# q and k of the attention stage turned by VectorE in 32x32 blocks instead of by TensorE

## The chip, the cores and the metric

The kernel runs on one core of a Trainium2 chip. The metric is the device time of one execution in microseconds; of several runs the median is given. A core has TensorE (PE; its weight loads are listed apart as PEld), VectorE (DVE), ScalarE (ACT), GpSimd (POOL) and SyncE (SP), which issues nearly all DMAs here. The DMAs run on 16 DMA engines of the core.

## The reference

```python
# q, k, v: (4, 12, 448, 64) fp32
scores = q @ k.T / sqrt(64) - log(448)
attn   = sigmoid(scores)
x      = (attn @ v)  -> (4 * 448, 768)          # tokens by features

# first mixture of experts: 8 experts, 768 -> 1024 -> 768
compute = x @ w_skip > 0
e       = argmax(x @ w_gate); g = softmax gate of e
out     = x;  out[compute] = x + g * relu(x @ w1[e]) @ w2[e]

# second mixture: experts by cosine with expert_emb / tau, every token computed
out = g2 * relu(x @ v1[e2]) @ v2[e2]
```

## The kernel before

It has two parts. The attention stage takes the first 178 us; the two mixtures of experts take the rest. The change is in the first part, and at the stores of the second.

**Attention.** The work is cut into 12 units (`duos`), each of one batch and four heads. A unit holds two pairs of heads, i = 0 and 1; j = 0 and 1 is the head in a pair. Head pairs lie in the two halves of the 128 partitions, so that q and k of a pair, once turned, are tiles `qT` and `kT` of 128 rows (two heads of 64 features) by 448 tokens. The keys of a head are cut into `NH` = 7 pieces of `KT` = 64. So a unit has 7 steps, and there are 84 steps in all, numbered g. In a step,

- `score(w, h)` runs four matmuls (both pairs, both heads) into one tile `psS`, and ScalarE takes the sigmoid of all of it into a tile `A`;
- `av(w, h)` runs four matmuls of the values with the tile `A` of two steps earlier (`LAG` = 2), summed in two PSUM tiles `psO` over the 7 steps. After the last step of a unit `take_x` moves them to `xT`, one by VectorE and one by ScalarE.

Each engine runs its instructions in the order in which the code issues them. SP has one queue. A DMA also waits for the DMA eight places ahead of it in this queue, since eight semaphores are used in turn.

**Loads.** `load_qk(w)` loads q and k of a unit by eight DMAs of 112 partitions x 4 pieces of 64 floats, `load_v(w)` the values by four DMAs of 64 partitions x 7 pieces of 64 floats. Tokens of q stand in the order (p c): partition p holds the four tokens 4p to 4p + 3. So the rows of the result stand in that order too, and the kernel's later index tables (`rid`) and stores follow it. The tiles `k`, `q` and `v` have two buffers each. In unit w, step 0 issues `load_qk(w + 1)` and step 2 issues `load_v(w + 1)`, whose buffer was that of unit w - 1.

**Transposes.** `prep(w, nm)` turns q or k of one unit: eight transposes of 112x128 by TensorE into two PSUM banks `ps_t`, which VectorE (i = 0) and ScalarE (i = 1) copy to `qT` or `kT`. For unit 0 this stands ahead of the first step; for unit w + 1 it stands in step 3 (k) and step 4 (q) of unit w, between `score` and `av`.

**Routing.** After the last unit of a batch the steps of the next unit also hold the first mixture's router for that batch (`route_stages`): matmuls, two groups of transposes and chains of small VectorE operations.

**Experts.** `dense` runs one expert over a whole batch; its weights come by SP in units of 256 columns (`load1`, `load2`, tile `r`). `finish` turns the result back to rows (tile `row`) and stores it: three batches by one DMA each of 112 rows of 12 KB, the last by two DMAs.

Of the kernel before, what the change touches and what calls it, by code (L numbers as in the profile page):

```python
# [10 lines left out]
F32 = mybir.dt.float32  # L11
F32R = mybir.dt.float32r
I32 = mybir.dt.int32
AF = mybir.ActivationFunctionType
# [7 lines left out]
def sigmoid_attention_moe_moe_kernel(  # L22
# [15 lines left out]
    nc = tc.nc  # L38
# [3 lines left out]
    P = 112  # L42
# [48 lines left out]
    def setup_steps(tmp):  # L91
        def loads():
            e = K["emb"] = tmp.tile([NE, DM], F32, tag="emb", name="emb", bufs=1)
            nc.gpsimd.dma_start(e, emb)
            r = K["wraw0"] = tmp.tile([128, ND, 9], F32, tag="wraw0", name="wraw0", bufs=1)
            nc.gpsimd.dma_start(r[:, :, :8], w_gate.rearrange("(c p) e -> p c e", p=128))
            with nc.allow_non_contiguous_dma(reason="768 floats"):
                nc.gpsimd.dma_start(r[:, :, 8:9], w_skip.rearrange("(c p o) -> p c o", p=128, o=1))
            it = K["itau"] = const("itau", [128, 2])
            nc.gpsimd.dma_start(it[:, 0:1], tau.to_broadcast([128, 1]))  # L100
            t = K["io_i"] = tmp.tile([128, 128], I32, tag="io_i", name="io_i", bufs=1)
            nc.gpsimd.iota(t, pattern=[[1, 128]], base=0, channel_multiplier=0)
            t = K["pci"] = tmp.tile([128, 8], I32, tag="pc_i", name="pc_i", bufs=1)
            nc.gpsimd.iota(t[:, 0:1], pattern=[[1, 1]], base=0, channel_multiplier=1)
            t = K["rid"] = tmp.tile([P, B, C], I32, tag="rid_i", name="rid_i", bufs=1)
            nc.gpsimd.iota(t, pattern=[[S, B], [1, C]], base=-SKIP, channel_multiplier=C)

        def emb_squares():
            ss = K["embss"] = tmp.tile([NE, 4], F32, tag="embss", name="embss", bufs=1)
# [414 lines left out]
    def attention():  # L524


        with ExitStack() as a:
            ld = a.enter_context(tc.tile_pool(name="ld", bufs=2, reuse_waits="tile"))
            wk = a.enter_context(tc.tile_pool(name="wk", bufs=2, reuse_waits="tile"))
            psS = a.enter_context(tc.tile_pool(name="psS", bufs=2, space=PSUM, reuse_waits="tile"))  # L530
            psO = a.enter_context(tc.tile_pool(name="psO", bufs=2, space=PSUM, reuse_waits="tile"))
            LDU, ST = {}, {}

            def load_qk(w):
                b, d = duos[w]
                t = {}
                for nm in "kq":
                    t[nm] = ld.tile([P, 2, C, 2 * D], F32, tag=nm, name=nm)
                for i in range(2):
                    for nm, src, pat in (("k", k, "(c p) d -> p c d"), ("q", q, "(p c) d -> p c d")):  # L540
                        for j in range(2):
                            nc.sync.dma_start(
                                t[nm][:, i, :, j * D : (j + 1) * D], src[b, 4 * d + 2 * i + j].rearrange(pat, c=C)
                            )
                LDU[w] = t

            def load_v(w):
                b, d = duos[w]
                t = LDU[w]["v"] = ld.tile([128, NH, 2, D], F32, tag="v", name="v")
                for i in range(2):  # L550
                    for j in range(2):
                        nc.sync.dma_start(
                            t[KT * i : KT * i + KT, :, j, :], v[b, 4 * d + 2 * i + j].rearrange("(h r) d -> r h d", r=KT)
                        )

            def prep(w, nm, which=(0, 1)):
                t = LDU[w][nm]
                if (w, nm) not in ST:
                    ST[w, nm] = wk.tile([128, 2, S], F32, tag=nm + "T", name=nm + "T")
                dst = ST[w, nm]  # L560
                got = {}
                for i in which:
                    ps = got[i] = bank("ps_t")
                    for c in range(C):
                        nc.tensor.transpose(ps[:, c * P : (c + 1) * P], t[:, i, c], ident[:P, :P])
                for i in which:
                    if i:
                        nc.scalar.activation(dst[:, i], got[i][:, :S], AF.Copy)
                    else:
                        nc.vector.tensor_copy(dst[:, i], got[i][:, :S])  # L570

            def score(w, h):
                kT, qT = ST[w, "k"], ST[w, "q"]
                at = wk.tile([128, 2, S], F32, tag="A", name="A", bufs=4)
                ps = psS.tile([128, 2, 512], F32, tag="psS", name="psS")
                for j in range(2):
                    r = slice(D * j, D * j + D)
                    for i in range(2):
                        nc.tensor.matmul(  # L579
                            ps[KT * i : KT * i + KT, j, :S], lhsT=kT[r, i, h * KT : (h + 1) * KT], rhs=qT[r, i],  # L580
                            start=True, stop=True,
                        )
                nc.scalar.activation(at, ps[:, :, :S], AF.Sigmoid, bias=bias, scale=1.0 / math.sqrt(D))  # L583
                ST[w, "a", h] = at

            def av(w, h):
                t = LDU[w]["v"]
                b, d = duos[w]
                if h == 0:
                    ST[w, "o"] = [  # L590
                        bank("psO") if w == N - 1 and i else psO.tile([128, 512], F32, tag="psO", name="psO") for i in range(2)
                    ]
                at = ST.pop((w, "a", h))
                for i in range(2):
                    r = slice(KT * i, KT * i + KT)
                    for j in range(2):
                        nc.tensor.matmul(  # L597
                            ST[w, "o"][i][D * j : D * j + D, :S], lhsT=t[r, h, j, :], rhs=at[r, j, :],
                            start=h == 0, stop=h == NH - 1,
                        )  # L600
                if h == NH - 1:
                    for i in range(2):
                        if w < N - 1 or not i:
                            take_x(b, 2 * d + i, ST[w, "o"][i])

            N = len(duos)
            G, LAG = N * NH, 2
            load_qk(0)
            load_v(0)
            for i in range(2):  # L610
                prep(0, "k", (i,))
                prep(0, "q", (i,))
            load_qk(1)
            load_v(1)
            todo = setup_steps(wk)
            late = {}
            for g in range(G + LAG):
                w, h = divmod(g, NH)
                if w > 0 and w + 1 < N and h == 0:
                    load_qk(w + 1)  # L620
                if w > 0 and w + 1 < N and h == LAG:
                    load_v(w + 1)
                if g < G:
                    score(w, h)
                if w + 1 < N and h in (3, 4):
                    prep(w + 1, "kq"[h - 3])
                if g >= LAG:
                    av(*divmod(g - LAG, NH))
                for f in [todo.pop(0)] if todo and g >= 2 else late.get(g, ()):
                    if f:  # L630
                        f()
                done = g - LAG + 1
                if done % NH == 0 and done > 0:
                    b, d = duos[done // NH - 1]
                    if d == NP // 2 - 1 and b < B - 1:
                        assert not todo
                        s1, s2, s3 = route_stages(R1, b, x_of(b))
                        todo = [None, s1, s2, None, s3]
                        if b == B - 2:
                            fs = [s1, s2, s3, lambda: gates(R1, 0, B - 1), lambda: plan_first(R1)] + first_steps()  # L640
                            at = [g + i for i in (2, 3, 5, 5, 7, 8, 8, 10, 10, 11, 14, 15, 16, 17)] + [G]
                            todo, late = [], schedule({}, fs, at)
            return ST[N - 1, "o"][1]
# [626 lines left out]
    def finish(j, b, end=False):  # L1270
# [20 lines left out]
        def tail():  # L1291
            if end:
                banks = BANKS + YS[1:5]
                for d0, n, m in ((0, 4, 1), (4, 2, 2)):
# [5 lines left out]
                        scaled(c, d0, n, t[:P, w : w + n * 128])  # L1300
                    cols = slice(d0 * 128, (d0 + n) * 128)
                    queue, bq = (nc.sync, b) if d0 == 0 else (nc.scalar, batch_of(j))
                    to = out.rearrange("(b p c) d -> p b c d", c=C, p=P)[:, ds(bq, 1), :, cols]
                    STORES.append(queue.dma_start(
                        to.rearrange("p o c d -> p (o c) d"),
                        ROW[:P].rearrange("p (c d) -> p c d", d=DM)[:, :, cols],
# [4 lines left out]
            for c in range(C):  # L1311
# [4 lines left out]
                        turn(t, (d - d0) * 128, c, d)  # L1316
                    scaled(c, d0, n, t[:P, : n * 128])
            nc.sync.dma_start(
                out.rearrange("(b p c) d -> p b (c d)", c=C, p=P)[:, ds(b, 1), :].rearrange("p o d -> p (o d)"), ROW[:P]
            )  # L1320

        return tail
# [88 lines left out]
```

## Time and profile before

| | us |
|---|---|
| median of 3 runs (620.62 to 622.90) | 621.38 |
| the profiled execution | 621.67 |
| its span, first to last instruction | 619.9 |
| attention stage, about | 178 |

All profile rows are of that one execution; their times count from the start of the span. What lies outside the span is 1.8 us. A busy time is the sum of an engine's instructions; a row's "idle before" is what its engine waited just ahead of it, with the one that released it. SPq rows are DMA issues: the time is that of the issuing, not of the transfer.

### The profile page before, as it was taken

The page shows a single profiled execution, that of the slowest core. Times are in us where ns is not written, and L with a number is a line of the kernel's source. Part 1 is how long each engine was busy: PE and PEld are TensorE (multiplying, and loading weights), DVE is VectorE, ACT ScalarE, POOL GpSimd, SP SyncE. Part 2 cuts the span into 40 slices and gives each one's busy share as a digit, 9 for nine tenths or more (in the row PEclk, how much of TensorE's full clock was granted, in tenths as well). Part 3 has the DMA queues.
Part 4 walks back from the last instruction along what each step waited for, and adds up shares of the span by engine and source line. Part 5 has one row for each costly group of instructions (what it writes and reads, how often), then busy time and mean ns, then how long its engine had stood idle before and what let it go on. Part 6 is the DMA issues. An engine that isn't in the chain of part 4 may idle for free. (4 is left out here: it accounts for less than half of the span.)

```text
span 619.9 us, 10285 instructions
## 1 busy us (share of the span) xinstructions
PE 597.1 (96%) x3882; PEld 444.0 (72%) x3882; DVE 286.6 (46%) x750; ACT 277.3 (45%) x455; POOL 7.5 (1%) x15
## 2 busy tenths in 40 slices
PE   6999999999999999999996999999999999999994
PEld 3444444444349998898865899988999799988882
DVE  0321312213475777674143965466635874442212
ACT  3656565665683245543014732383228323532111
POOL 2010000000000000000000000000000000000000
PEclk9999999999999999999997999999999999999998
DMA  9454454433724233333255305080506241373243
GB/s 159 106 113 104 90 114 98 91 90 90 233 71 135 92 114 105 104 103 103 102 209 174 137 1 204 1 287 7 205 0 211 82 145 61 92 252 103 82 173 95
DMA packets 102189, 73.38 MB, mean 118 GB/s; under 512 B 68082, under 2 KB 93126, under 8 KB 101776
## 3 DMA queue, kind: packets, MB, share of 16 engines
q1 hardware_dynamic: 101456, 71.91, 38.8%
q8 instruction: 39, 0.64, 0.5%
q10 hardware_dynamic: 464, 0.46, 0.3%
q14 instruction: 38, 0.31, 0.2%
q0 software_dynamic: 192, 0.07, 0.1%
HBM read 66.90 MB, written 5.70 MB: 117 GB/s over the span
## 5 line engine op out<-in xcount | busy, mean ns | idle before, releaser
L754 PE MATMUL bank<-xs,h 128*128 128x448 f32 x288 | 108.7, 377 | 6.6 <-DVEq L1256 5.8
L583 ACT ACTIVATE A<-psS,bias 128x896 f32<-128x896 f32 x84 | 84.6, 1007 | 55.9 <-PE psS L579 55.3
L754 PE MATMUL y<-hh,h 128*128 128x448 f32 x288 | 108.5, 377 | 0.0
L756 PE MATMUL bank<-xs,l 128*128 128x448 f32 x288 | 106.3, 369 | 0.7 <-DVE l L745 0.7
L774 ACT ACTIVATE hh<-bank 128x448 fp32r<-128x448 f32 x48 | 26.0, 541 | 180.5 <-PE bank L756 165.8
L755 PE MATMUL bank<-xs,h 128*128 128x448 f32 x288 | 106.5, 370 | 0.0
L755 PE MATMUL y<-hl,h 128*128 128x448 f32 x288 | 105.7, 367 | 0.0
L756 PE MATMUL y<-hh,l 128*128 128x448 f32 x288 | 105.6, 367 | 0.0
L745 DVE TENSOR_TENSOR l<-r,h 128x512 fp32r<-128x512 f32 (+1 forms) x115 | 85.3, 791 | 4.5 <-ACT h L744 2.7
L775 DVE SCALAR_TENSOR_TENSOR hl<-bank,hh 128x448 fp32r<-128x448 f32 x48 | 29.9, 622 | 116.2 <-ACT hh L774 115.8
L579 PE MATMUL psS<-qT,kT 64*64 64x448 f32 x672 | 82.9, 555 | 0.0
L597 PE MATMUL psO<-A,v 64*64 64x448 f32 x672 | 81.4, 548 | 1.0 <-DVE pl L360 1.0
L744 ACT ACTIVATE h<-r 128x512 fp32r<-128x512 f32 (+1 forms) x115 | 74.6, 710 | 0.0
L754 PEld LDWEIGHTS bank<-xs,h 128*128 128x128 f32 x288 | 54.8, 190 | 16.1 <-issue 7.1
L754 PEld LDWEIGHTS y<-hh,h 128*128 128x128 f32 x288 | 54.1, 188 | 8.2 <-issue 2.9
L756 PEld LDWEIGHTS bank<-xs,l 128*128 128x128 f32 x288 | 54.8, 190 | 6.0 <-DVE l L745 1.1
L755 PEld LDWEIGHTS bank<-xs,h 128*128 128x128 f32 x288 | 54.8, 190 | 4.4
L756 PEld LDWEIGHTS y<-hh,l 128*128 128x128 f32 x288 | 54.1, 188 | 4.9
L755 PEld LDWEIGHTS y<-hl,h 128*128 128x128 f32 x288 | 54.2, 188 | 4.6 <-issue 0.2
L579 PEld LDWEIGHTS psS<-qT,kT 64*64 64x64 f32 x672 | 27.8, 136 | 34.9 <-issue 28.2
L597 PEld LDWEIGHTS psO<-A,v 64*64 64x64 f32 x672 | 24.2, 133 | 35.3 <-issue 22.2
L522 DVE COPY xT<-psO 128x448 f32<-128x448 f32 x12 | 7.4, 619 | 42.6 <-PE psO L597 42.6
(248 smaller groups left out, 478.2 us busy)
## 6 DMA issues: line engine op xcount, KB each, us to landing
r<-in_moe_w_dram SPq DMA_DIRECT2D x62, 768.0 KB, 5.9
k<-in_k_dram SPq DMA_DIRECT2D x48, 112.0 KB, 3.0
q<-in_q_dram SPq DMA_DIRECT2D x48, 112.0 KB, 3.0
v<-in_v_dram SPq DMA_DIRECT2D x48, 112.0 KB, 3.1
out_dram<-row SPq DMA_DIRECT2D x3, 1344.0 KB, 6.8
out_dram<-row SPq DMA_DIRECT2D x1, 896.0 KB, 5.5
stg<-in_moe_w_dram SPq DMA_DIRECT2D x1, 768.0 KB, 8.3
row<-in_moe_w_dram SPq DMA_DIRECT2D x1, 768.0 KB, 9.7
```

Of the source, the lines that this page charges most:

```text
L522: nc.vector.tensor_copy(x, ps[:, :S])
L579: nc.tensor.matmul(ps[KT * i : KT * i + KT, j, :S], lhsT=kT[r, i, h * KT : (h + 1) * KT], rhs=qT[r, i], start=True, stop=True,)
L583: nc.scalar.activation(at, ps[:, :, :S], AF.Sigmoid, bias=bias, scale=1.0 / math.sqrt(D))
L597: nc.tensor.matmul(ST[w, "o"][i][D * j : D * j + D, :S], lhsT=t[r, h, j, :], rhs=at[r, j, :], start=h == 0, stop=h == NH - 1,)
L744: nc.scalar.activation(dst_h, src, AF.Copy)
L745: nc.vector.tensor_sub(dst_l, src, dst_h.bitcast(F32))
L754: nc.tensor.matmul(ps, lhsT=ah, rhs=bh, start=first, stop=False)
L755: nc.tensor.matmul(ps, lhsT=ah, rhs=bl, start=False, stop=False)
L756: nc.tensor.matmul(ps, lhsT=al, rhs=bh, start=False, stop=last)
L774: nc.scalar.activation(a, ps[:, :S], AF.Relu)
L775: nc.vector.scalar_tensor_tensor(l, ps[:, :S], 0.0, a.bitcast(F32), op0=ALU.max, op1=ALU.subtract)
```

## The change

The transposes of units 1 to 11 move from TensorE to VectorE. VectorE's transpose turns each 32x32 block where it stands, so the DMAs put the blocks in place: of q and k a DMA fills 32 partitions (a row r of a block in each) with 14 pieces of 32 floats, and eight such DMAs fill a tile of 128 x 2 x 448. One `nc.vector.transpose` then gives `qT`, two give `kT` (in an order of keys that fits the new order of v). `load_qk` issues 16 DMAs a unit instead of 8. `load_v` issues 8 instead of 4, each of 32 partitions with one piece of 448 floats (1792 bytes). The loads of q and k are issued two units ahead. Unit 0 keeps TensorE's transposes (`load_first`, `turn_first`), with k loaded to 32 partitions and turned in 14 pieces. Tokens stand in plain order, (c p) instead of (p c).

```diff
-            nc.gpsimd.iota(t, pattern=[[S, B], [1, C]], base=-SKIP, channel_multiplier=C)
+            nc.gpsimd.iota(t, pattern=[[S, B], [P, C]], base=-SKIP, channel_multiplier=1)
...
+            def load_first():
+
+                t = LDU[0] = {}
+                t["k"] = ld.tile([32, 2, 2 * NH, 2 * D], F32, tag="k0", name="k0", bufs=1)
+                t["q"] = ld.tile([P, 2, C, 2 * D], F32, tag="q0", name="q0", bufs=1)
+                for i in range(2):
+                    for nm, src, pat in (("k", k, "(p c) d -> p c d"), ("q", q, "(c p) d -> p c d")):
+                        for j in range(2):
+                            p = 32 if nm == "k" else P
+                            nc.sync.dma_start(
+                                t[nm][:, i, :, j * D : (j + 1) * D], src[0, 2 * i + j].rearrange(pat, p=p)
+                            )
...
-                for nm in "kq":
-                    t[nm] = ld.tile([P, 2, C, 2 * D], F32, tag=nm, name=nm)
-                for i in range(2):
-                    for nm, src, pat in (("k", k, "(c p) d -> p c d"), ("q", q, "(p c) d -> p c d")):
-                        for j in range(2):
+                t = LDU[w] = {nm: ld.tile([128, 2, S], F32, tag=nm, name=nm) for nm in "kq"}
+                for nm, src, pat in (("k", k, "(r t) d -> r t d"), ("q", q, "(t r) d -> r t d")):
+                    for i in range(2):
+                        for g in range(4):
+                            rows, f = slice(32 * g, 32 * g + 32), g % 2 * 32
                             nc.sync.dma_start(
-                                t[nm][:, i, :, j * D : (j + 1) * D], src[b, 4 * d + 2 * i + j].rearrange(pat, c=C)
+                                t[nm][rows, i].rearrange("r (t d) -> r t d", d=32),
+                                src[b, 4 * d + 2 * i + g // 2, :, f : f + 32].rearrange(pat, r=32),
                             )
...
-                t = LDU[w]["v"] = ld.tile([128, NH, 2, D], F32, tag="v", name="v")
+                t = LDU[w]["v"] = ld.tile([128, 2, NH, D], F32, tag="v", name="v")
                 for i in range(2):
                     for j in range(2):
-                        nc.sync.dma_start(
-                            t[KT * i : KT * i + KT, :, j, :], v[b, 4 * d + 2 * i + j].rearrange("(h r) d -> r h d", r=KT)
-                        )
+                        for e in range(2):
+                            at = KT * i + 32 * e
+                            nc.sync.dma_start(
+                                t[at : at + 32, j],
+                                v[b, 4 * d + 2 * i + j].rearrange("(r e h) d -> r e h d", e=2, h=NH)[:, e],
+                            )
...
-                    for c in range(C):
-                        nc.tensor.transpose(ps[:, c * P : (c + 1) * P], t[:, i, c], ident[:P, :P])
...
+            def turn(w, nm):
+                dst = ST[w, nm] = wk.tile([128, 2, S], F32, tag=nm + "T", name=nm + "T")
+                src = LDU[w][nm]
+                if nm == "q":
+                    nc.vector.transpose(dst.rearrange("p i s -> p (i s)"), src.rearrange("p i s -> p (i s)"))
+                    return
+                for i in range(2):
+                    nc.vector.transpose(
+                        dst[:, i].rearrange("p (h e r) -> p e h r", e=2, r=32), src[:, i].rearrange("p (e h r) -> p e h r", e=2, r=32)
+                    )
...
-            load_qk(0)
+            load_first()
             load_v(0)
             for i in range(2):
-                prep(0, "k", (i,))
-                prep(0, "q", (i,))
+                turn_first("k", i)
+                turn_first("q", i)
             load_qk(1)
             load_v(1)
+            load_qk(2)
...
-                if w > 0 and w + 1 < N and h == 0:
-                    load_qk(w + 1)
+                if 0 < w < N - 2 and h == 0:
+                    load_qk(w + 2)
...
                 if w + 1 < N and h in (3, 4):
-                    prep(w + 1, "kq"[h - 3])
+                    turn(w + 1, "kq"[h - 3])
```

How the rows move is shown at three places. A row of the order names the line, the operation, what is written and read, the shape, and how often it stands there in a row. First SP's queue from its first DMA to the load of v for unit 2, before:

```order
L542 DMA k<-in_k_dram 112x4x64 x2
L542 DMA q<-in_q_dram 112x4x64 x2
L542 DMA k<-in_k_dram 112x4x64 x2
L542 DMA q<-in_q_dram 112x4x64 x2
L552 DMA v<-in_v_dram 64x7x64 x4
```

and of the change, up to v of unit 2:

```order
L543 DMA k_129<-in_k_dram 32x14x64 x2
L543 DMA q_130<-in_q_dram 112x4x64 x2
L543 DMA k_129<-in_k_dram 32x14x64 x2
L543 DMA q_130<-in_q_dram 112x4x64 x2
L568 DMA v<-in_v_dram 32x448 x8
L556 DMA k<-in_k_dram 32x14x32 x8
L556 DMA q<-in_q_dram 32x14x32 x8
L568 DMA v<-in_v_dram 32x448 x8
L556 DMA k<-in_k_dram 32x14x32 x8
L556 DMA q<-in_q_dram 32x14x32 x8
L556 DMA k<-in_k_dram 32x14x32 x8
L556 DMA q<-in_q_dram 32x14x32 x8
L568 DMA v<-in_v_dram 32x448 x8
```

Before, these five rows repeat once for every unit. Now the values of unit 2 stand behind q and k of units 2 and 3, and from there on each unit has 16 DMAs of q and k two units ahead and 8 of v one unit ahead.

Second, TensorE in unit 0, from the first matmuls of `score` on, before:

```order
L579 MATMUL psS<-qT,kT 64x448 x4
L565 MATMUL ps_t<-ident,k 128x112 x8
L597 MATMUL psO<-A,v 64x448 x4
L579 MATMUL psS<-qT,kT 64x448 x4
L565 MATMUL ps_t<-ident,q 128x112 x8
L597 MATMUL psO<-A,v 64x448 x4
```

and of the change, from the start of the program:

```order
L580 MATMUL ps_t<-ident,k_129 128x32 x14
L580 MATMUL ps_t<-ident,q_130 128x112 x4
L580 MATMUL ps_t<-ident,k_129 128x32 x14
L580 MATMUL ps_t<-ident,q_130 128x112 x4
L604 MATMUL psS<-qT,kT 64x448 x12
L622 MATMUL psO<-A,v 64x448 x4
L604 MATMUL psS<-qT,kT 64x448 x4
L622 MATMUL psO<-A,v 64x448 x4
```

The two groups of eight transposes in a unit are gone, and ahead of the first step k has 14 small ones for each i where it had four.

Third, VectorE behind the set-up of the constants, in unit 2 and on, before:

```order
L522 COPY xT<-psO 128x448
L570 COPY kT<-ps_t 128x448
L570 COPY qT<-ps_t 128x448
```

and now:

```order
L522 COPY xT<-psO 128x448
L593 STREAM_TRANSPOSE kT<-k 128x2x7x32 x2
L590 STREAM_TRANSPOSE qT<-q 128x896
```

The transposes stand where the copies stood, between two moves of `xT`; they wait for a DMA instead of for TensorE.

## Rows read from the trace of the kernel before

**Rows 1.** The page: busy us (share of the span) and instructions of each engine.

```profile
PE 597.1 (96%) x3882; PEld 444.0 (72%) x3882; DVE 286.6 (46%) x750; ACT 277.3 (45%) x455; POOL 7.5 (1%) x15
```

**Rows 2.** Busy us by window, one unit; the last three columns are clock, DMA share, GB/s.

```profile
71.00:84.00 13.00, 13.00 (x130) 5.93 (x130) 1.88 (x3) 8.35 (x10) 0.00 (x0) 1.00 0.48 107
```

**Rows 3.** Who waited for whom, 0 to 240 us: total us, times, longest.

```profile
ACT A L583 <- PE psS L579: 55.3, 68, 1.9
...
PEld psO L597 <- DVE xT L522: 6.6, 9, 0.7
...
PE ps_t L565 <- DMA k<-in_k_dram: 3.7, 1, 3.7
```

**Rows 4.** Time line of TensorE in one unit: start us, us, operation.

```profile
74.38 0.93 PE L579 MATMUL psS<-qT,kT 64*64 64x448 f32 x8
75.24 0.98 PE L565 MATMUL ps_t<-ident,q 112*128 112x112 f32 x8
...
76.96 0.93 PE L579 MATMUL psS<-qT,kT 64*64 64x448 f32 x8
...
78.46 0.93 PE L579 MATMUL psS<-qT,kT 64*64 64x448 f32 x8
```

**Rows 5.** Time line of SP's DMA issues, 80 to 165 us: start us, us for all of xcount.

```profile
83.24 3.80 SPq L552 DMA_DIRECT2D v<-in_v_dram  x4
...
112.42 2.65 SPq L552 DMA_DIRECT2D v<-in_v_dram  x4
115.11 1.15 SPq L542 DMA_DIRECT2D k<-in_k_dram  x2
116.30 1.26 SPq L542 DMA_DIRECT2D q<-in_q_dram  x2
117.61 1.15 SPq L542 DMA_DIRECT2D k<-in_k_dram  x2
...
125.43 2.65 SPq L552 DMA_DIRECT2D v<-in_v_dram  x4
...
138.44 2.65 SPq L552 DMA_DIRECT2D v<-in_v_dram  x4
...
154.61 2.65 SPq L552 DMA_DIRECT2D v<-in_v_dram  x4
159.45 0.44 SPq L476 DMA_DIRECT2D r<-in_moe_w_dram  x1
160.09 0.39 SPq L481 DMA_DIRECT2D r<-in_moe_w_dram  x1
160.68 0.37 SPq L476 DMA_DIRECT2D r<-in_moe_w_dram  x1
```

**Rows 6.** Groups by line (busy us, mean ns), and the instructions of line 169.

```profile
L522 DVE COPY xT<-psO 128x448 f32<-128x448 f32 x12 | 7.4, 619 | 42.6 <-PE psO L597 42.6
...
L147 DVE TENSOR_SCALAR tri<-io,pc 128x128 f32<-128x128 f32 x1 | 0.3, 279 | 0.0
...
L169 PE MATMUL ps_emb<-ident,emb x6: 201/202/223, 38.8 to 39.1; 8*128 8x8 f32 x6
```

**Rows 7.** Time line of the first unit: SP's issues, and TensorE's first score.

```profile
5.62 2.68 SPq L552 DMA_DIRECT2D v<-in_v_dram  x4
...
27.41 2.65 SPq L552 DMA_DIRECT2D v<-in_v_dram  x4
...
9.72 3.21 PE L579 MATMUL psS<-qT,kT 64*64 64x448 f32 x12
```

**Rows 8.** DMA queues (packets, MB, share), 30 to 150 us, then 320 to 400; issues to landing.

```profile
q1 hardware_dynamic: 49288, 12.19, 45.1%
...
v<-in_v_dram SPq DMA_DIRECT2D x33, 112.0 KB, 3.0
...
q1 hardware_dynamic: 5544, 8.55, 30.1%
```

**Rows 9.** Time line of TensorE where unit 10 begins its values.

```profile
156.26 1.08 PE L597 MATMUL psO<-A,v 64*64 64x448 f32 x8 [0.99 <-DVE pl L360]
```

More of the change, by code (lines that the diff above doesn't have):

```diff
@@ L534, in load_qk @@
             def load_qk(w):
                 b, d = duos[w]
-                t = {}
-                for nm in "kq":
-                    t[nm] = ld.tile([P, 2, C, 2 * D], F32, tag=nm, name=nm)
-                for i in range(2):
-                    for nm, src, pat in (("k", k, "(c p) d -> p c d"), ("q", q, "(p c) d -> p c d")):
-                        for j in range(2):
+                t = LDU[w] = {nm: ld.tile([128, 2, S], F32, tag=nm, name=nm) for nm in "kq"}
[3 more added lines that the diff above has]
+                            rows, f = slice(32 * g, 32 * g + 32), g % 2 * 32
@@ L542, in load_qk @@
                             nc.sync.dma_start(
-                                t[nm][:, i, :, j * D : (j + 1) * D], src[b, 4 * d + 2 * i + j].rearrange(pat, c=C)
+                                t[nm][rows, i].rearrange("r (t d) -> r t d", d=32),
+                                src[b, 4 * d + 2 * i + g // 2, :, f : f + 32].rearrange(pat, r=32),
                             )
-                LDU[w] = t
             def load_v(w):
                 b, d = duos[w]
-                t = LDU[w]["v"] = ld.tile([128, NH, 2, D], F32, tag="v", name="v")
+                t = LDU[w]["v"] = ld.tile([128, 2, NH, D], F32, tag="v", name="v")
@@ L550, in load_v @@
                 for i in range(2):
                     for j in range(2):
-                        nc.sync.dma_start(
-                            t[KT * i : KT * i + KT, :, j, :], v[b, 4 * d + 2 * i + j].rearrange("(h r) d -> r h d", r=KT)
-                        )
[L556 to L563, printed above, removed]
-                    for c in range(C):
-                        nc.tensor.transpose(ps[:, c * P : (c + 1) * P], t[:, i, c], ident[:P, :P])
[L566 to L570, printed above, removed]
+                        for e in range(2):
[4 more added lines that the diff above has]
+                            )
@@ new lines, in turn_first @@
+            def turn_first(nm, i):
+                if i == 0:
+                    ST[0, nm] = wk.tile([128, 2, S], F32, tag=nm + "T", name=nm + "T")
+                ps = bank("ps_t")
+                n, p = (2 * NH, 32) if nm == "k" else (C, P)
+                for c in range(n):
+                    o = c % NH * KT + c // NH * 32 if nm == "k" else c * P
+                    nc.tensor.transpose(ps[:, o : o + p], LDU[0][nm][:, i, c], ident[:p, :p])
+                if i:
+                    nc.scalar.activation(ST[0, nm][:, i], ps[:, :S], AF.Copy)
+                else:
+                    nc.vector.tensor_copy(ST[0, nm][:, i], ps[:, :S])
@@ L597, in av @@
                         nc.tensor.matmul(
-                            ST[w, "o"][i][D * j : D * j + D, :S], lhsT=t[r, h, j, :], rhs=at[r, j, :],
+                            ST[w, "o"][i][D * j : D * j + D, :S], lhsT=t[r, j, h, :], rhs=at[r, j, :],
                             start=h == 0, stop=h == NH - 1,
@@ L1302, in tail @@
                     queue, bq = (nc.sync, b) if d0 == 0 else (nc.scalar, batch_of(j))
-                    to = out.rearrange("(b p c) d -> p b c d", c=C, p=P)[:, ds(bq, 1), :, cols]
+                    to = out.rearrange("(b c p) d -> p b c d", c=C, p=P)[:, ds(bq, 1), :, cols]
                     STORES.append(queue.dma_start(
@@ L1318, in tail @@
             nc.sync.dma_start(
-                out.rearrange("(b p c) d -> p b (c d)", c=C, p=P)[:, ds(b, 1), :].rearrange("p o d -> p (o d)"), ROW[:P]
+                out.rearrange("(b c p) d -> p b c d", c=C, p=P)[:, ds(b, 1)].rearrange("p o c d -> p (o c) d"),
+                ROW[:P].rearrange("p (c d) -> p c d", d=DM),
             )
```

## The prediction

> **What bounds the kernel now.** The page comes first: TensorE is busy for 597.1 us of a span of 619.9, VectorE and ScalarE for less than half [rows 1]. So time is won only where TensorE loses work, and lost only where it is made to wait. The change touches the attention stage, the first 178 us. The busy times by window show what it is there: in one unit of 13.00 us TensorE is busy for all of it at the full granted clock (1.00), VectorE for 1.88, ScalarE for 8.35, the DMA engines at a share of 0.48 [rows 2]. The list of waits agrees: ScalarE waits for TensorE all the time (55.3 us), and TensorE's own waits are small (6.6 us for nine moves of `xT`, 3.7 us for the first `k`) [rows 3].
>
> The time line of one unit gives TensorE's prices. A step (`score` and `av`) that holds no transposes takes from 76.96 to 78.46, 1.50 us; the step with the eight transposes of q takes from 74.38 to 76.96, 2.58 us [rows 4]. So one group of eight transposes costs TensorE 1.08 us.
>
> SP's issues are the second thing to read, since the change doubles their number. SP issues one unit's twelve DMAs without a break: four of v in 2.69 us start to start, a pair of k in 1.19 and a pair of q in 1.31 us; that is 7.7 us of the unit's 13.0, and the next v, which waits for TensorE to let its buffer go, comes 13.01 us after the last [rows 5]. Spare time on SP is about 5 us in a unit, and that is what the change spends.
>
> **The change, part by part.**
>
> *TensorE loses 22 groups of transposes* (k and q of units 1 to 11). At 1.08 us that is 23.8 us, and all of it lies on the path, because TensorE has no idle time in these steps [rows 2, 4]. ScalarE loses two copies in each unit, which frees nothing that anything waits for [rows 3].
>
> *VectorE gets the transposes.* No row shows a 32x32 transpose. The nearest are a copy of 448 elements in each partition, 0.62 us, and an operation of 128, 0.28 us, so 1.06 ns for each further element [rows 6]. By these the one instruction of 896 takes 1.10 us, or 1.24 as two copies, and two of 448 take 1.24. I take 2.4 us in a unit where two copies took 1.24. Cover: VectorE is idle for 11 of 13 us [rows 2], and `turn` stands three steps before its result is needed. Only at four times this price would `xT` move late behind it. I take nothing; without that cover it would be the 1.1 us more in each of 11 units, 12 us, the upper bound.
>
> *The first unit* keeps TensorE's transposes, but k goes in 14 pieces of 32 rows. The second k and the second q run back to back before the first score at 9.72 [rows 7], so ten more pieces count once. Eight transposes add 1.08 us, 0.135 each [rows 4], so 1.35 us is the upper bound; those of `ps_emb`, six between 38.8 and 39.1, come every 0.06 us [rows 6]. I take 0.6, since pieces of 32 rows are nearer to these.
>
> *SP issues 24 DMAs in a unit instead of 12*: 16 of q and k (32 partitions by 14 pieces of 128 bytes), 8 of v (32 pieces of 1792 bytes). This decides the forecast. No row shows these shapes. Lower bound: the weights, 0.37 to 0.44 us an issue, 0.41 with the shortest gap of 0.04 between q and k [rows 5]. Upper bound: today's v, 0.67 us start to start. What separates the rows? Not the number of pieces: `r` at line 476 has 768 pieces and takes no longer than the one at line 481 with 256, while k, q and v have 448 and take more than either. What weights have and today's q, k and v lack is that each partition's bytes lie in one run in SBUF (k, q and v are written to every other 256 bytes). The new q, k and v tiles are filled in one run in each partition too. So I take the weights' price, 0.43 us with the gap to the next issue: 10.3 us in a unit. Some stretches are longer by about 1.1 us (v 3.80 at 83.24 for 2.65) [rows 5]; up to 100 us there is about one in a unit, and an SP that never rests will meet each. That makes 11.4 us in a unit. TensorE's units become 13.0 - 2.2 = 10.8 us, and 14 where routing lies (v's first issues at 125.43 and 138.44 are 13.01 us apart, those at 138.44 and 154.61 are 16.17) [rows 5], 11.7 in the mean. So SP just keeps up.
>
> The Trainium skill says otherwise of issue time ("Perfetto Trace Analysis", § DMA Instruction — HWDGE): the profiled window of such an instruction is the generating of its descriptors, so that it should grow with their number. By that rule q and k would stay at 0.62, the first rival below. The two weight rows speak against it.
>
> *The start loses some*, because v(2) stands in SP's queue behind q and k of both units 2 and 3. First eight DMAs until 5.6 [rows 7]; then 8 v, 16, 8 v, 16, 16 and 8 v, 72 issues at 0.43, are 31.0 us; with two long ones 38.8; landing about 2.6 after the issue's end (3.0 from its start [rows 8]): 41.4. TensorE wants v(2) at 36.6: unit 0's `av` ended at 27.4, where v's issue was released [rows 7], plus 0.6, minus 2.2, plus one unit of 10.8. A stall of 4.8 us, and one of about 1 us at unit 3; then unit 3's routing lets SP catch up. 5.8 us in all.
>
> *The 16 DMA engines.* 49288 packets, nearly all of 256 bytes, filled 45.1% of 16 engines' 120 us: 17.6 ns each. In a stretch with weights alone, 5544 packets of 1542 bytes on average took 30.1% of 80 us: 69 ns [rows 8]. A line through both gives 13 ns at 128 bytes and 79 at 1792. So a unit's 7168 small and 256 large packets take 5.8 + 1.3 = 7.1 us; at 17.6 ns for the small ones 9.2. Both are below SP's 11.4. Nothing is added.
>
> The Trainium skill warns of this ("DMA: Bandwidth & Descriptors", § Specifications): transfers under 512 bytes fall below line rate. The trace agrees for 256 bytes (17.6 ns, a quarter of the 1 to 3 KB packets' price for a sixth of the bytes); the engines still have room.
>
> *Tokens in plain order* changes the iota, the order inside lists, and three stores from 12 KB pieces to 3 KB ones. No engine reads those stores back, and the last one, on which the kernel's end hangs, keeps its shape: nothing, either way.
>
> Sum, against the profiled execution's 621.67 us: 621.7 - 23.8 + 0.6 + 5.8 = 604.3. The median of the runs, 621.38, lies 0.3 below that execution, so 604.
>
> **The rivals.**
>
> *Q and k stay at the price of today* (0.615 us start to start), because 448 pieces must be made whatever they look like; v falls to 0.43. For it: k, q and v all have 448 pieces. Against it: the weights. SP then bounds the stage. Up to v(10), which the first `av` of unit 10 needs: 5.6 + 176 x 0.615 + 88 x 0.43 = 151.7, with 11 long issues 163.7, landed 166.3. Today that `av` starts at 156.26 [rows 9]; unit 10 then saves 2.2 us. 10.0 - 2.2 = 7.8 us slower, 629; without long issues 617.
>
> *Few partitions are dear* (slower than before): v, with 64 partitions, is the dearest row, so 32 may cost at least as much, all 24 at 0.67. Then 88 x 0.24 = 21 us more, 651. Against it: the weights with 128 partitions and q with 112 differ by as much, 0.37 and 0.63, at nearly the same number of partitions [rows 5].
>
> The point from which SP decides: zero change needs that `av` at 158.5, which leaves (158.5 - 2.6 - 12 - 5.6) / 264 = 0.52 us an issue.
>
> *The doubled queue is hidden wholly*: 0.41 us an issue and no long ones. Then only 23.8 comes off and 0.6 on: 598.
>
> **How the numbers follow.** The forecast with its near variants (issues at 0.41 to 0.50 us; at 0.50 that `av` of unit 10 comes at 5.6 + 264 x 0.50 + 12 + 2.6 = 152.2, so 6.3 us come off in all, 615): 0.58. Issues near the break-even: 0.08. Q and k at today's price: 0.22, of which 0.02 without long issues. All at v's price: 0.12. About 0.5% (3 us) is what a measurement of this kernel can tell from no change. Faster 0.60, same 0.08, slower 0.32. The forecast's own range is 598 to 615; to leave out no more than 2 in 10 it must take in the first rival: 597 to 634.
>
> **What the profile will show.** Right: no transposes on TensorE after the first score, steps of 1.50 us throughout; SP's q and k issues at about 0.4 us in blocks of 16; a wait of TensorE for v near 37 us and few after 55; first `av` of unit 10 near 141; VectorE's transposes about 1.1 us and no wait of TensorE on them. Wrong: SP solid with q and k at 0.6 us, TensorE waiting for v in every unit; or VectorE at several us a transpose, with `xT` moved late behind it. A packet of 128 bytes above 23 ns would also undo the sum: (11.7 - 1.3) x 16 / 7168.

## The result and the profile after

The changed kernel takes 630.50 us (median of four runs, 629.07 to 630.63) beside 621.17 of the kernel before (four runs, 620.62 to 622.90): ratio 1.0138, interval 1.0122 to 1.0154. The forecast was 604, range 597 to 634. The kernel is 1.4% slower where 2.8% faster was forecast.

The page: TensorE lost the work that was to go, 156 matmuls of [rows 1], and yet the span grew.

```profile
span 627.3 us, 10150 instructions
...
PE 594.0 (95%) x3726; PEld 460.3 (73%) x3726; DVE 296.7 (47%) x761; ACT 267.8 (43%) x433; POOL 7.5 (1%) x15
```

The time line of TensorE at four places: the second half of the first unit's k, the first score, the first `av` of unit 10 (156.26 in [rows 9]) and the first matmul behind the attention stage.

```profile
9.05 1.67 PE L580 MATMUL ps_t<-ident,k 32*128 32x32 f32 x14 [0.91 <-DMA k<-in_k_dram]
...
11.59 3.25 PE L604 MATMUL psS<-qT,kT 64*64 64x448 f32 x13
...
166.49 1.29 PE L622 MATMUL psO<-A,v 64*64 64x448 f32 x8 [0.99 <-DVE pl L360]
...
187.35 0.47 PE L780 MATMUL bank<-xs,h 128*128 128x448 f32 x1
```

The same last matmul in the kernel before:

```profile
178.77 0.47 PE L754 MATMUL bank<-xs,h 128*128 128x448 f32 x1
```

The stage ends 8.6 us later, and from there to the span's end both need nearly the same (619.9 - 178.8 = 441.1, 627.3 - 187.4 = 439.9). So the loss lies in the attention stage, and this mark, the first matmul behind it, is what the experiments are read by.

SP's issues there, by the time line of its queue (start us, us for all of xcount):

```profile
35.16 5.22 SPq L556 DMA_DIRECT2D k<-in_k_dram  x8
40.48 4.44 SPq L556 DMA_DIRECT2D q<-in_q_dram  x8
45.03 3.75 SPq L568 DMA_DIRECT2D v<-in_v_dram  x8
48.88 5.24 SPq L556 DMA_DIRECT2D k<-in_k_dram  x8
...
73.70 3.67 SPq L568 DMA_DIRECT2D v<-in_v_dram  x8
77.47 5.23 SPq L556 DMA_DIRECT2D k<-in_k_dram  x8
82.80 5.31 SPq L556 DMA_DIRECT2D q<-in_q_dram  x8
88.21 3.67 SPq L568 DMA_DIRECT2D v<-in_v_dram  x8
```

Each block starts about 0.1 us after the end of the one before: where [rows 5] had some 5 us of rest in a unit, SP has none. From v to v is 14.51 us; TensorE's work for a unit without transposes is some 10.8 (measured below), or 14.0 in every third unit, where routing lies (97.98 - 83.97 between two first issues of v in the kernel "merged, all quarters" below).

Each line's issues (count, then shortest, median and longest ns):

```profile
L556 SPq DMA_DIRECT2D k<-in_k_dram x88: 566/621/630, 10.4 to 154.7; - x88
L556 SPq DMA_DIRECT2D q<-in_q_dram x88: 312/477/2017, 15.7 to 159.1; - x88
...
L568 SPq DMA_DIRECT2D v<-in_v_dram x96: 310/419/1442, 5.8 to 168.0; - x96
```

With a gap of 0.044 us to the next, k costs 0.665, q 0.522 and v 0.463 us. So k is dearer than q by 30%, though both are 32 rows by 14 pieces of 128 bytes and have the same size. They differ only in which tokens the pieces are.

Who waits for it, 0 to 190 us (total us, times, longest):

```profile
DVE kT L593 <- DMA k<-in_k_dram: 12.4, 4, 6.2
PEld psO L622 <- DMA v<-in_v_dram: 7.6, 10, 0.9
DVE qT L590 <- DMA q<-in_q_dram: 6.5, 2, 4.1
...
PE psO L622 <- DMA v<-in_v_dram: 5.7, 5, 1.9
```

VectorE waits for k and q before it can turn them, TensorE for v. Before, TensorE was busy for all of a unit [rows 2]. The windows add the clock (the column behind the engines):

```profile
30.00:40.00 10.00, 6.98 (x72) 5.07 (x64) 3.60 (x16) 4.73 (x5) 0.59 (x1) 1.00 0.56 90
40.00:45.00 5.00, 3.29 (x30) 1.49 (x30) 0.85 (x3) 1.86 (x3) 1.66 (x1) 0.83 0.63 101
45.00:50.00 5.00, 3.14 (x13) 0.85 (x6) 2.65 (x6) 1.01 (x1) 0.00 (x0) 0.50 0.51 115
50.00:60.00 10.00, 10.00 (x90) 6.78 (x91) 0.00 (x0) 4.29 (x5) 0.00 (x0) 0.82 0.58 92
```

TensorE, idle a third of 30 to 45 us, falls to a granted clock of 0.50, its lower level (1.2 GHz), and comes back only in the next window: a stall there costs more than its own length.

VectorE's transposes, by line (busy us, mean ns | idle time before them):

```profile
L593 DVE STREAM_TRANSPOSE kT<-k 128x448 f32<-128x448 f32 x22 | 13.0, 624 | 12.4 <-DMA k<-in_k_dram 12.4
L590 DVE STREAM_TRANSPOSE qT<-q 128x896 f32<-128x896 f32 x11 | 12.0, 1092 | 7.1 <-DMA q<-in_q_dram 6.5 <-DMA v<-in_v_dram 0.5
```

The list of transfers (count, KB each, median us from issue to landing; 3.0 for v in [rows 8]):

```profile
v<-in_v_dram SPq DMA_DIRECT2D x96, 56.0 KB, 2.0
k<-in_k_dram SPq DMA_DIRECT2D x88, 56.0 KB, 2.5
q<-in_q_dram SPq DMA_DIRECT2D x88, 56.0 KB, 2.4
```

Transposes and these landings are as cheap as forecast or cheaper; the issue is the first suspect. SP's own waits are small: the list of its queue up to the last v (168 us) has 1.3 us for earlier DMAs and 1.5 us for TensorE and VectorE. So the wait for the DMA eight places ahead does not set its pace.

### The profile page after: what moved, and what is told of

The parts are those of the page before. It is cut to its first block, busy times and chain, and to the rows that moved or that the text cites. A ratio compares the mean times of both kernels' runs of the same rounds, so it can differ in the third digit from the quotient of the medians.

```text
span 627.3 us, 10150 instructions
## 1 busy us (share of the span) xinstructions
PE 594.0 (95%) x3726; PEld 460.3 (73%) x3726; DVE 296.7 (47%) x761; ACT 267.8 (43%) x433; POOL 7.5 (1%) x15
## 5 line engine op out<-in xcount | busy, mean ns | idle before, releaser
L622 PE MATMUL psO<-A,v 64*64 64x448 f32 x672 | 119.6, 554 | 7.0 <-DMA v<-in_v_dram 5.7
L604 PE MATMUL psS<-qT,kT 64*64 64x448 f32 x672 | 109.4, 569 | 3.6 <-DVE embss L202 3.0
L622 PEld LDWEIGHTS psO<-A,v 64*64 64x64 f32 x672 | 50.2, 136 | 46.3 <-issue 26.7
L604 PEld LDWEIGHTS psS<-qT,kT 64*64 64x64 f32 x672 | 45.6, 139 | 30.0 <-issue 23.7
```

Of the source, the lines that this page charges most:

```text
L604: nc.tensor.matmul(ps[KT * i : KT * i + KT, j, :S], lhsT=kT[r, i, h * KT : (h + 1) * KT], rhs=qT[r, i], start=True, stop=True,)
L622: nc.tensor.matmul(ST[w, "o"][i][D * j : D * j + D, :S], lhsT=t[r, j, h, :], rhs=at[r, j, :], start=h == 0, stop=h == NH - 1,)
```

## The experiments

Two theories. **A**: SP's issues bound the stage, each at a price that depends on the DMA, so whatever takes issue time off SP brings TensorE's saving back. **B**: the small packets bound it, in the 16 DMA engines or in landing, so a lighter SP gains nothing. Beside them stood the order of SP's queue, and the stall near 47 us with its clock. All kernels but the first run the changed kernel's VectorE transposes; "unit" is SP's time from v to v, "mark" the first matmul behind the attention stage.

| kernel | SP issues in a unit | mark, us | time, us | ratio to before (interval) |
|---|---|---|---|---|
| before | 12 | 178.8 | 621.2 | 1 |
| changed | 24 | 187.4 | 630.5 | 1.0138 (1.0122 to 1.0154) |
| k's pattern as q's | 24 | 174.9 | 599.9, not comparable | 0.9641 (0.9612 to 0.9671) |
| v by four DMAs | 20 | 177.0 | 616.4 | 0.9894 (0.9854 to 0.9934) |
| k like q: both | 20 | 162.8 | 604.6 | 0.9733 (0.9714 to 0.9753) |
| v ahead of q and k | 24 | 181.0 | 622.1 | 1.0019 (1.0005 to 1.0033) |
| v on GpSimd's queue | 16 | 162.4 | 611.0 | 0.9842 (0.9819 to 0.9864) |
| k like q, v on GpSimd | 16 | 158.1 | 599.6 | 0.9652 (0.9613 to 0.9692) |
| k like q, v ahead | 20 | 158.3 | 598.8 | 0.9639 (0.9618 to 0.9660) |
| merged | 12 | 207.6 | 649.0 | 1.0441 (1.0420 to 1.0461) |
| merged, old pairing | 12 | 155.0 | 596.6 | 0.9593 (0.9564 to 0.9622) |
| merged, all quarters | 12 | 155.7 | 597.7 | 0.9621 (0.9597 to 0.9644) |
| k like q, split | 36 | 244.0 | 684.4 | 1.1022 (1.0996 to 1.1049) |

### k like q

```diff
-("k", k, "(r t) d -> r t d"), ("q", q, "(t r) d -> r t d")
+("k", k, "(t r) d -> r t d"), ("q", q, "(t r) d -> r t d")
```

k's row r now holds tokens 32t + r, as q's does. v goes back to four DMAs of 64x7x64, since the keys then need it so, one transpose of 896 does for k, and the first unit's k is loaded in four pieces of 112 rows as before.

> k is loaded with q's access pattern (token t*32+r instead of r*14+t in row r) and turned by one transpose of 896 columns like q; v goes back to four DMAs of 64x7x64 as in the kernel before. Theory A (SyncE's queue, at a price per DMA that depends on its source pattern, bounds the attention stage): 16 x 0.522 + 4 x 0.67 = 11.0 us a unit instead of 13.2, with the long issue 12.2 instead of 14.4; eight units or so that ran at SyncE's pace gain about 2 us each, so the first product of unit 10 with v comes near 150 (166.5 in the changed kernel, 156.3 in the kernel before) and the time is 605 to 615 us. Rival B (the DMA engines or the landing of the small packets bound it, not the issue): the same number of 128-byte packets and twice as many for v, so no gain, 628 to 635 us. Rival C (the stall of 1.9 us for v of unit 2 and the clock that falls behind it is what costs): v still stands behind q and k of units 2 and 3 there, so at most 3 us of gain.

604.6 us, just under theory A's range; the first `av` of unit 10 comes at 142.47, earlier than the 150 worked out. B's range is out. The unit falls to 11.94 us (74.08 to the next v at 86.02), with seven times the pieces for v (4 x 448 instead of 8 x 32; the expectation's "twice" is wrong) and the same for q and k:

```profile
65.59 4.21 SPq L556 DMA_DIRECT2D k<-in_k_dram  x8
69.90 4.07 SPq L556 DMA_DIRECT2D q<-in_q_dram  x8
74.08 2.62 SPq L566 DMA_DIRECT2D v<-in_v_dram  x4
...
86.02 2.62 SPq L566 DMA_DIRECT2D v<-in_v_dram  x4
```

TensorE waits once more at the start (3.24 us for v of unit 2) and then hardly. Rival C, that the stall alone costs, is out too: the stall is still there and 26 us are gained.

### Its two parts apart

In one kernel only k's pattern is changed, in the other only v's DMAs. Each mixes keys and values, as its expectation says.

> Of the changed kernel only k's source pattern is another: piece t of row r is token 32t+r, as for q, instead of token 14r+t. DMAs, pieces, bytes and every instruction on the other engines stay; the scores are then of other keys than v's rows, so the output isn't the reference's. Theory A (SyncE's issue bounds and its price hangs on the source pattern): 8 issues a unit go from 0.665 to 0.522, 1.14 us a unit, eight to nine units at SyncE's pace, so the first product of unit 10 with v comes near 156 (166.5 in the changed kernel) and the time is 617 to 623 us. Rival B (the pieces' own transfer or landing bounds): no gain, 628 to 633 us.

> Of the changed kernel only v is loaded as in the kernel before, by four DMAs of 64x7x64 instead of eight of 32x448; k and q stay. v's rows are then other tokens than the keys, so the output isn't the reference's. Theory A (SyncE's issue bounds): v goes from 8 x 0.463 = 3.7 us a unit to 4 x 0.672 = 2.7, a gain of 1.0 us a unit, and the time is 618 to 624 us, though v's packets are seven times as many. Rival B (packets and engines bound): slower than the changed kernel, over 632 us.

The pattern alone: k's issue falls from a median of 621 to 477 ns, a unit from 14.51 to 13.20 us (68.50 to 81.70), the mark comes 12.4 us earlier. Issues of k and v there:

```profile
68.50 3.68 SPq L568 DMA_DIRECT2D v<-in_v_dram  x8
72.28 4.02 SPq L556 DMA_DIRECT2D k<-in_k_dram  x8
...
81.70 3.67 SPq L568 DMA_DIRECT2D v<-in_v_dram  x8
```

v alone: a unit of 13.64 us, the mark 10.4 us earlier, and 616.4 us, 1.6 under its range. With k's pattern the first `av` of unit 10 comes at 153.91 (156 expected), but the total, 599.9, can't be read: other keys route other tokens, and a stage near the end then has less to do. The matmuls of line 928 in that kernel (count, then shortest, median and longest ns):

```profile
L928 PE MATMUL bank<-ident,stg x24: 270/272/299, 257.6 to 279.0; 128*112 128x128 f32 x24
```

and in the changed one, where as many again come near the end:

```profile
L928 PE MATMUL bank<-ident,stg x48: 270/272/320, 269.6 to 568.3; 128*112 128x128 f32 x48
```

The mark lies ahead of that. By it the parts add up: 12.4 + 10.4 = 22.8 us, and the kernel with both gained 24.5, which contains the first unit's old k load too (its first score comes at 10.57, 1.0 us earlier than in the changed kernel).

### v ahead of q and k

```diff
-if 0 < w < N - 2 and h == 0:
-    load_qk(w + 2)
 if w > 0 and w + 1 < N and h == LAG:
     load_v(w + 1)
+if 0 < w < N - 2 and h == LAG:
+    load_qk(w + 2)
```

> Of the changed kernel only the order on SyncE's queue is another: v of the next unit is issued ahead of q and k of the unit after it, both at step 2 of a unit, from unit 1 on. Theory A (the rate bounds): SyncE still needs 14.4 us a unit, so the waits move from v to q and k and the time stays within 4 us of the changed kernel's 630. Rival E (the order bounds: v behind sixteen q and k issues is what TensorE waits for): the waits for v go and the time falls to 605 to 615 us.

622.1 us: between both. The unit is as long as ever, so the rate is not what gained:

```profile
78.00 4.72 SPq L568 DMA_DIRECT2D v<-in_v_dram  x8
82.82 5.22 SPq L556 DMA_DIRECT2D k<-in_k_dram  x8
88.14 4.21 SPq L556 DMA_DIRECT2D q<-in_q_dram  x8
92.44 3.67 SPq L568 DMA_DIRECT2D v<-in_v_dram  x8
```

My bound of 4 us for theory A was wrong. SP as the bound still allows one gain: the v that TensorE needs last has 16 issues less ahead of it, 16 x 0.59 = 9.5 us, once, not in each unit; the mark moved by 6.3. So order matters, and by this reading by a constant, which no run tests by itself. The same swap with k like q:

> The kernel with k loaded like q, all on SyncE, and v of the next unit issued ahead of q and k of the unit after it. SyncE needs 12.2 us a unit for its 20 issues either way, TensorE 10.7. Theory A: the rate is still a little short, but each unit's v has 16 fewer issues ahead of it, so the waits go except near the start: 599 to 603 us (604.6 with v behind). If order doesn't matter, 603 to 606 us.

598.8 us, 0.2 under theory A's range, the mark 4.5 us earlier: order matters here too.

### v on GpSimd's queue

```diff
-nc.sync.dma_start(
+(nc.gpsimd if w else nc.sync).dma_start(
```

> Of the changed kernel only v's eight DMAs of units 1 to 11 go to GpSimd's queue. Theory A: SyncE is left with 8 x 0.665 + 8 x 0.522 = 9.5 us a unit, 10.7 with the long issue, under TensorE's 11.7; GpSimd has 8 x 0.8 = 6.4 us a unit beside little else; the time is 600 to 610 us. Rival B (the DMA engines or the packets): no gain, 628 to 635 us. Rival D (GpSimd's issue is held up by something of its own, so that v is late there): TensorE waits for v and the time is over 620 us.

> The kernel with k loaded like q, and v's four DMAs of units 1 to 11 on GpSimd's queue. SyncE is left with 16 x 0.522 = 8.4 us a unit, 9.5 with the long issue, under TensorE's 10.7. The wait of 3.2 us for v of unit 2 and the 4 us of half clock behind it go: 598 to 602 us (604.6 with v on SyncE). If k and q are still late at the start, or GpSimd's issue makes v late, 603 to 606 us. The whole forecast of TensorE's saving, 23.8 us, would be 597.5.

The marks, 162.4 and 158.1, are theory A's: SP with 16 issues lets TensorE go. The second takes 599.6 us, within its range. The first takes 611.0 us, over its range, since from its mark to the end it needs 446.1 us where the other kernels with their full work need 438 to 441. A drain of GpSimd's queue holds the end. Its instructions of line 1433 in that kernel (shortest, median, longest ns):

```profile
L1433 POOLq DRAIN  x3: 46/103/7667, 600.0 to 608.2; - x3
```

and in the changed one:

```profile
L1433 POOLq DRAIN  x3: 40/109/1685, 624.3 to 627.0; - x3
```

The difference, 6.0 us, is nearly that between the two ways from the mark to the end (446.1 and 439.9). With 44 loads of v on that queue (k like q) the longest drain is 2682 ns, but without any it is nearly as long in kernels of that family, 2574 in the one with merged loads and the old pairing:

```profile
L1423 POOLq DRAIN  x3: 40/109/2574, 590.6 to 594.5; - x3
```

So the 88 loads are paid for at the end, the 44 are not, as far as can be seen; why, no run shows.

### Fewer and more issues for the same pieces

From here the kernels go on from k like q. One DMA brings a row group's pieces of two heads (32x28 pieces), 8 for q and k instead of 16; to have them side by side, the two halves of the score are then other heads:

```diff
-    r = slice(D * j, D * j + D)
-    for i in range(2):
+    for i in range(2):
+        r, x = (slice(D * i, D * i + D), j) if w else (slice(D * j, D * j + D), i)
```

> As the kernel in which k is loaded like q, and besides one DMA brings a row group's piece of two heads (32x28 pieces of 128 bytes) instead of one: 8 issues for q and k in a unit instead of 16, the same bytes and packets; the score's halves are other heads, the result is the same. Theory A1 (price per DMA): 8 x 0.52 + 4 x 0.67 = 6.9 us a unit on SyncE, which is then idle at the end of each unit, TensorE is the bound at 11.7 us a unit, and the time is 598 to 606 us. Theory A2 (price per piece that a DMA describes): 8 x 1.04 + 4 x 0.67 = 11.0 us, the time within 3 us of the kernel with k like q. Rival B (the DMA engines): no gain on the changed kernel, 628 to 635 us.

649.0 us, outside all ranges, and not because of DMAs: TensorE is busy all the time at the full clock, and a unit takes it 15.79 us. The cause that I then supposed is in the next expectation:

> The kernel that merged q's and k's DMAs (8 issues of 32x28 pieces a unit instead of 16) but with the score's matmuls paired as in the kernel before: two matmuls on one half of the rows, then two on the other, so that four follow each other on the four quarters of the array. In the merged kernel each quarter that was used came twice in four matmuls and the other two never. The heads are then mixed between score and v, so the output isn't the reference's. If the pairing was what made the merged kernel's unit 15.8 us long (649 us), the unit falls to 10.7 and, as SyncE has only 8 x 0.65 + 4 x 0.67 = 7.9 us of issues, the time is 598 to 604 us. If the merged DMAs were what slowed it, it stays over 640 us. If a merged DMA's price were that of its pieces (1.04), SyncE would need 11.0 us and the time be that of the kernel with k like q, 604.

One unit of the merged kernel by windows (TensorE's busy us first):

```profile
100.00:115.79 15.79, 15.79 (x116) 6.06 (x116) 2.64 (x3) 7.04 (x9) 0.00 (x0) 1.00 0.69 88
```

and one with the old pairing:

```profile
72.98:83.70 10.72, 10.72 (x116) 6.52 (x115) 2.64 (x4) 7.37 (x9) 0.00 (x0) 1.00 1.00 130
```

The same 116 matmuls at the same clock, 15.79 against 10.72 us; the two kernels differ only in the order in which the score's matmuls take the halves of the rows. The time, 596.6 us, is 1.4 under the range for the pairing as the cause. And with SP no longer in the way, the mark comes 23.8 us ahead of the kernel before, the saving that the prediction worked out:

```profile
154.98 0.47 PE L770 MATMUL bank<-xs,h 128*128 128x448 f32 x1
```

(The late stage that shrank with k's pattern has its 48 matmuls here, so this time can be read.) The same in full, with the second head of a pair in the other half of the columns:

> The reference in full: k loaded like q, q's and k's DMAs of two neighbouring heads merged (8 issues a unit of 32x28 pieces), v by four DMAs, all on SyncE. The second head of a pair stands in the other half of the array's columns, so that four matmuls that follow each other use all four quarters, in the score and in the product with v. If the issue count was all that TensorE waited for: a unit of 10.7 us, the first product of unit 10 with v at 134.7 as in the kernel with mixed heads, and 595 to 598 us. If the new order of the quarters (00, 01, 11, 10) costs TensorE anything, its unit is longer than 10.7 us and the time over 600 us.

597.7 us, in the range for the issue count. A unit is 10.85 us from v to v; by the same measure it is 10.82 with the old pairing, so this order of the quarters costs TensorE next to nothing. SP rests again (v at 62.26, 73.11 and 83.97, four of its 12 issues each):

```profile
62.26 2.62 SPq L565 DMA_DIRECT2D v<-in_v_dram  x4
64.98 2.35 SPq L555 DMA_DIRECT2D k<-in_k_dram  x4
67.42 2.94 SPq L555 DMA_DIRECT2D q<-in_q_dram  x4
73.11 2.62 SPq L565 DMA_DIRECT2D v<-in_v_dram  x4
```

And the other way, each q and k DMA in two:

> The kernel with k loaded like q, each q and k DMA split into two of seven pieces a row: 32 issues a unit for q and k instead of 16, same pieces and bytes. If the price is mostly one for each DMA (0.45 us or more for half of the pieces): 32 x 0.45 + 4 x 0.67 = 17.1 us a unit on SyncE and more with the long issue, so 645 to 675 us. If it is one for each piece (0.26 us for half of them): 11.0 us a unit and the time within 4 us of 604.6.

684.4 us, above even that range. Sixteen half DMAs take 7.89 us, eight whole ones took 4.21; the unit is 19.47:

```profile
61.37 2.63 SPq L567 DMA_DIRECT2D v<-in_v_dram  x4
64.09 7.89 SPq L557 DMA_DIRECT2D k<-in_k_dram  x16
72.08 8.65 SPq L557 DMA_DIRECT2D q<-in_q_dram  x16
80.84 2.62 SPq L567 DMA_DIRECT2D v<-in_v_dram  x4
```

The price is mostly one for each DMA: median 444 ns with 7 pieces a row, 477 with 14, and with 28 (all quarters) 562 for k and 734 for q. Those two have the same shape and the same source pattern, so pieces and pattern are not all that sets it. The DMA engines' share there is 0.92 to 1.00 in a unit, against 0.65 in k like q; whether that holds q's issues up, no run shows.

## Why the prediction was wrong

**The step that failed** is the price of SP's issues: "So I take the weights' price, 0.43 us with the gap to the next issue". For v it was near (0.463). For q it is 0.522 and for k 0.665; in a unit 8 x (0.665 + 0.522 + 0.463) = 13.2 us instead of 10.3, 14.5 with the long issue. The reason given, that weights are cheap because each partition's bytes lie in one run in SBUF, fell: k's and q's tiles are filled alike, and k costs 0.14 us more. The source pattern makes that, since the pattern alone took it away; why neighbours are dear, no run shows. The weights' rows were also no rows of a queue that never rests: each stands 0.2 us or more behind the issue before it [rows 5]. In the changed kernel the issues of v and q behind a gap of over 0.3 us took 0.31 to 0.33 us, most of the others 0.42 and 0.48. The Trainium skill ("Perfetto Trace Analysis", § DMA Instruction — HWDGE) puts the generating of the descriptors into the profiled window. From that I drew that an issue grows with their number, and set it aside. The trace has it grow, but by 33 ns from 7 to 14 pieces a row, on a base of 0.44.

**The first rival** was right in what happens, SP bounding the stage, and not in its reason: it had q and k stay dear for their 448 pieces, and half of the pieces cost 444 ns instead of 477. It put the first `av` of unit 10 at 166.3 and the time at 629; they are 166.49 and 630.5. That they meet so closely is luck, since its parts were off in opposite directions: q and k 0.594 in the mean instead of 0.615 (3.7 us less for 176), v 0.463 instead of 0.43 (2.9 more for 88). The break-even of 0.52 us an issue holds too: at 13.2 / 24 = 0.55 the mark is 8.6 us behind the kernel before, at (16 x 0.522 + 8 x 0.463) / 24 = 0.50, k's pattern alone, 3.9 us ahead. The second rival's 651 was summed wrongly: it left out 176 x 0.055 = 9.7 us for q and k at v's price, so it stood for some 660. Its reason fell too: all three have 32 partitions, and only k came near 0.67.

**TensorE's 23.8 us** were right where SP rests: 178.8 - 155.0. A unit falls from 13.01 to 10.82 us from v to v, by 2.19 where 2.16 was forecast. That the tenth is met is chance, since that kernel's first score comes 0.7 us later (10.43) than before.

**VectorE** was right: 1.09 us for 896 columns (1.10 forecast) and 0.62 for 448, 2.3 us in a unit (2.4). Where a transpose came late in the changed kernel, it had itself waited for k or q (12.4 and 6.5 us).

**The first unit** costs more than 0.6: the first score comes at 11.59 instead of 9.72. The pieces cost about what was forecast (14 in 1.67 us where four took 0.98). What the forecast put at nothing is k's later landing: 5.45 us until the first k is there, where it was 3.74, and 0.91 of waiting at the second.

**The start** was right in its place and short in size, by the same price: v(2) was put at 41.4, and TensorE gets the first of it at 47.70, so a stall that was to be 5.8 us grew, with a clock of 0.50 behind it. On k like q, v ahead gives 4.5 us of mark and v elsewhere 4.7, this stall with them.

**The DMA engines** were right: 54% of the unit from 73.70 to 88.21 is 7.8 us (7.1 to 9.2 forecast), and k like q has seven times the pieces for v, the same for q and k, and is faster. Their room is not fixed: in the merged kernel with the old pairing the same pieces as in k like q fill them to a share of 1.00.

## What to carry to other kernels

Before work is moved from an engine to "more, smaller DMAs", count the issues of a unit times their price back to back, and compare that with the unit as it will be after the saving, not as it is. A queue that issues without a break is a bound like an engine, though the page shows it nowhere as busy. Choose the pattern on the DRAM side (12.4 us of mark here) and merge issues (neighbouring heads in one DMA, 7.8 us more on k like q); a load that waits on SP behind another unit's loads is better issued ahead of them.

## What the runs showed of the hardware

- An issue that follows another at once costs more than one after a rest: v's shortest is 310 ns and its median 419, q's 312 and 477, and in the changed kernel every issue of v and q under 340 ns stands behind a gap of over 0.3 us. A price read from scattered issues is too low for a queue that never rests.
- The same bytes in the same number of pieces cost 477 or 621 ns to issue, by the tokens that a row's pieces are.
- About once in 16 us an issue takes 0.9 to 2.0 us (q's longest 2017 ns). In the trace of the changed kernel the ten of the attention stage lie within 0.4 us of the ten packets of 16 KB that the instruction queue moves there; which causes which is not shown.
- Four 64x64 matmuls that follow each other on four different quarters of the array take half the time of four on two quarters: a step is 1.50 us with the first, 0.75 each for `score` and `av`, and 2.25 with the second, where only the score's four were so placed.
- GpSimd's closing drain took 7.67 us in a kernel with 88 loads of v on its queue; with 44 it took 2.68, and with none 1.67 to 2.57 where the late stage was whole.
